# A GpSimd add moved behind the next causal select, and matmuls cut into shorter pieces at two places

## The chip, the cores and the metric

The kernel runs on one core of a Trainium2 chip. The core has five engines that run their own instruction streams and meet at semaphores: TensorE (PE in the rows; PEld is its weight load), VectorE (DVE), ScalarE (ACT), GpSimd (POOL) and SyncE (SP, which here only starts DMAs). The metric is the device time of one execution in microseconds. A run is timed on its own, and one execution is also recorded by the hardware profiler.

## The reference, cut to what matters

Two stages follow each other. The first is attention for 4 batches and 8 heads over 768 positions of 64 numbers, where each query may see 6 of the 24 chunks of 32 keys: those with the highest bound on the score.

```python
ub = np.sum(np.maximum(q * k_min, q * k_max), axis=-1)      # bound of each query on each chunk
ub = np.where(causal, ub, -1e9)
top_chunks = np.argsort(ub, axis=-1)[..., -6:]
scores = scale * np.matmul(q, k.transpose(0, 1, 3, 2))
scores = np.where(sel & (pos[:, None] >= pos[None, :]), scores, -1e9)
attn = np.exp(scores - np.max(scores, axis=-1, keepdims=True))
attn = attn / (np.sum(attn, axis=-1, keepdims=True) + 1e-09)
out = np.matmul(attn, v)
```

The second routes the 3072 rows of 512 to one of 8 experts each (argmax of `x @ w_gate`), keeps at most 80 rows an expert, those with the highest gate, and writes `gate * (relu(x @ w1[e]) @ w2[e])` for the rows kept and zeros elsewhere.

## The kernel before, in words

**Pairs and steps.** Two heads of one batch are worked on together, so there are 16 pairs, `i` = 0 to 15 (`NP` = 16, `NPB` = 4 pairs a batch). The causal half of a pair's score matrix is cut into six steps (`STEPS`). A step is one or two blocks of keys (128 keys on the partitions) against a range of queries (the columns). For each step PE makes the scores (`score_mm`, L572, and L560 for keys in halves of 64) and adds a large negative number for chunks not chosen (`flags`, L594). ACT then takes the exponential out of PSUM into the SBUF buffer `EXB` (L604), and POOL sets the upper triangle of the diagonal block to zero (`select`, L656 or L653).

**Sums.** The softmax denominators come from `ES`, the sum of the exponentials over key blocks. POOL adds step by step (`fold`, L672, with the pieces listed in `ADDS`), and DVE adds a last part (`own_fold`, L678 to L684). `fold(3)` is one add of 512 columns: it sums the step 2 and step 3 exponentials of queries 512 to 767 into `ES`. `sums` (L730, L753) brings `ES` to PSUM on PE once the pair after it has begun, and `sums_out` (L739 to L742) takes reciprocals on DVE.

**Values.** `values` (L717) multiplies the exponentials by `v`: 12 blocks a pair, for each of the two heads, into one PSUM tile `OB`, the heads in its two partition halves. A float32 matmul stands in the trace as two MATMULs and two LDWEIGHTS, so 12 blocks for two heads are 48 MATMULs. In most pairs the order of the blocks is that of `AVS`: the fifth block needs step 4's exponentials after the select, and the last needs step 5's.

**Three kinds of pairs.** `mid(i)` is 1 to 14. `short(i)` holds for 1, 2, 3, 4, 5, 8, 9 and 13: they take keys in halves and run steps 4 and 5 in another order. The other middle pairs are 6, 7, 10, 11, 12 and 14. `direct(i)` holds for 5, 9 and 13. In a short pair `fold(3)` already stands behind step 4's select; in the others it stands right behind step 3's (`folds`, L686 to L701).

**Order.** It is written out by hand: the loop over `i` issues scores, sums of the pair before, folds, values and the preparation of the next pairs, and each engine works through its own list in that order. Routing work of a batch (gates, ranks, tables) is put between the pairs of the next batch, mostly on DVE: in pairs 6, 10 and 14 `rank_hot`, `gate_digits` and the columns of a table (L1072 to L886), whose matmul `table` (L1085) stands in the next pair, for pair 14 in the same pair.

**The end.** For pair 15, `sums_last` (L792) makes the sums straight from `EXB`. The values are given in two calls around `last_row` (L895), which turns the gates for ranking; then counts (L976), the choice of rows, gathers of chosen rows from DRAM by POOL's indirect DMAs (L1366), and the experts' matmuls (L1457 up, L1483 down). The first gathered rows are turned at L1000.

**Splits.** `score_mm` cuts the 512 columns of steps 0 and 1 in two pieces of 256 where `(i - 1) * 2 + st < 10`, that is in pairs 1 to 5.

## Time and profile before

| | |
|---|---|
| time, median of 3 runs | 270.26 us (270.12 to 270.38) |
| the profiled execution | 270.17 us, of which the span of the program's instructions is 268.2 us |
| PE busy | 256.0 us (95%), 4152 MATMULs |
| DVE busy | 214.8 us (80%) |
| POOL busy | 207.6 us (77%) |
| ACT busy | 155.4 us (58%) |
| chain that ended last | PE 73%, POOL 11%, DVE 5%, DMA 4% |

Times in the rows are microseconds from the span's start. In the timeline a row is a run of instructions of one kind: start, length, engine, line, operation, tiles, shapes and count, and in brackets how long the engine sat idle before it and what ended that. PE works on several instructions at a time and the ends of its matmuls are modelled, so its idle time in brackets is a lower bound.

### The profile page before, as it was taken

What the parts mean: (1) busy time and instruction counts of PE and PEld (TensorE: products, weight loads), DVE (VectorE), ACT (ScalarE), POOL (GpSimd) and SP (SyncE); (2) the same over time, 40 slices, a digit from 0 to 9 for tenths busy, and PEclk for the clock granted to TensorE, in tenths of its full rate; (3) what the DMA queues carried; (4) which work ended last, traced back from release to release, by engine and by line L of the source; (5) the groups of instructions that cost most, each with busy time, mean ns of one, the idle gap of its engine ahead of it and who ended that gap; (6) DMA issues with size and microseconds to landing.
All of it is one profiled execution on the core that took longest, in us unless ns stands there. A gap on an engine that the chain in (4) does not pass through costs nothing.

```text
span 268.2 us, 9821 instructions
## 1 busy us (share of the span) xinstructions
PE 256.0 (95%) x4152; PEld 167.2 (62%) x4152; DVE 214.8 (80%) x587; ACT 155.4 (58%) x243; POOL 207.6 (77%) x291
## 2 busy tenths in 40 slices
PE   7799999999999999999999999999999999988993
PEld 7367676767676565666665666666556557664663
DVE  6878787687989988859899889999998998953242
ACT  2286757575777654657776456564865576841220
POOL 6068959895999798969997999888998942725852
PEclk9999999999999999999999999999999999999999
DMA  9979999999999999997999889969999991911771
GB/s 148 173 128 165 142 293 195 298 222 222 151 200 205 226 160 197 206 221 147 164 186 222 150 147 210 212 112 295 287 243 218 215 190 9 197 44 47 152 150 65
DMA packets 148618, 48.38 MB, mean 180 GB/s; under 512 B 131583, under 2 KB 138870, under 8 KB 148512
## 3 DMA queue, kind: packets, MB, share of 16 engines
q1 hardware_dynamic: 113552, 23.23, 44.5%
q0 software_dynamic: 9936, 18.64, 36.9%
q10 hardware_dynamic: 25088, 5.90, 10.9%
q8 instruction: 32, 0.52, 0.8%
q14 instruction: 10, 0.08, 0.1%
HBM read 57.03 MB, written 11.01 MB: 254 GB/s over the span
## 4 chain that ended last, share of the span: by engine, by line
PE 73%; POOL 11%; DVE 5%; DMA 4%; ACT 3%; issue 2%; ACTq 1%; DVEq 0%
PE OB L717 22%; PE SC L572 13%; POOL ES L672 8%; PE SC L560 7%; PE SC L594 5%; PE OB L1483 4%; PE SC L1457 4%; PE MM L483 4%; PE MM L753 3%; ACT EXB L604 3%; DMA qn<-x_rows,idx 3%; PE MM L730 2%; POOL EXB L656 2%; PE OB L801 2%; DMA qn<-in_q_dram 1%
## 5 line engine op out<-in xcount | busy, mean ns | idle before, releaser
L604 ACT ACTIVATE EXB<-SC 128x1024 f32<-128x1024 f32 (+2 forms) x87 | 81.2, 947 | 35.9 <-PE SC L594 14.4
L672 POOL TENSOR_TENSOR ES<-ES,EXB 128x512 f32<-128x512 f32 (+1 forms) x76 | 80.4, 1060 | 5.1
L717 PE MATMUL OB<-EXB,vn 128*64 128x256 f32 (+2 forms) x640 | 69.6, 365 | 0.8 <-POOL EXB L656 0.7
L572 PE MATMUL SC<-qT,kT 64*128 64x256 f32 (+3 forms) x356 | 61.2, 450 | 0.1
L717 PEld LDWEIGHTS OB<-EXB,vn 128*64 128x64 f32 x640 | 42.9, 137 | 23.3 <-issue 7.5
L672 POOL TENSOR_TENSOR ES<-EXB 128x512 f32<-128x512 f32 (+1 forms) x29 | 45.0, 1551 | 1.8
L594 PE MATMUL SC<-unsT,ind 64*128 64x320 bf16 (+9 forms) x286 | 34.9, 303 | 0.4
L572 PEld LDWEIGHTS SC<-qT,kT 64*128 64x128 f32 x356 | 29.1, 187 | 8.9 <-issue 4.4
L725 ACT ACTIVATE oT<-OB 128x512 f32<-128x512 f32 (+1 forms) x32 | 15.7, 490 | 31.6 <-PE OB L717 31.6
L656 POOL TENSOR_SCALAR_AFFINE_SELECT EXB<-EXB 128x256 f32<-128x256 f32 x63 | 27.5, 442 | 5.5 <-ACT EXB L604 5.5
L656 POOL TENSOR_SCALAR_AFFINE_SELECT ES<-EXB 128x256 f32<-128x256 f32 x15 | 7.3, 484 | 22.3 <-PE MM L753 14.9
L594 PEld LDWEIGHTS SC<-unsT,ind 64*128 64x128 bf16 (+1 forms) x286 | 12.3, 100 | 17.9 <-issue 8.2
L560 PE MATMUL SC<-qT,kT 64*64 64x256 f32 (+5 forms) x256 | 21.7, 436 | 0.0
L450 DVE STREAM_TRANSPOSE qT<-qn 128x768 f32<-128x768 f32 x16 | 15.5, 971 | 5.8 <-PE SC L594 5.0
L454 ACT ACTIVATE rq<-qT 128x768 f32<-128x768 f32 x16 | 13.5, 845 | 9.7 <-DVE qT L450 9.2
L460 DVE STREAM_TRANSPOSE kT<-kn 128x768 f32<-128x768 f32 x16 | 15.5, 968 | 1.4 <-DMA kn<-in_k_dram 1.2
L462 DVE TENSOR_REDUCE kmm<-kT 128x24 f32<-128x768 f32 x16 | 15.3, 953 | 0.5
L465 DVE TENSOR_REDUCE kmx<-kT 128x24 f32<-128x768 f32 x16 | 15.1, 941 | 0.0
L497 DVE MAX8 top<-MM 128x8 f32<-128x8 f32 (+4 forms) x160 | 14.6, 164 | 0.6
L828 DVE TENSOR_TENSOR xp<-OB,rden 128x768 bf16<-128x768 f32 x14 | 13.3, 953 | 0.4
L739 DVE STREAM_TRANSPOSE MM<-MM 128x192 f32<-128x192 f32 x16 | 6.3, 394 | 8.3 <-PE MM L753 8.0
L753 PE MATMUL MM<-ES,onc 128*32 128x192 f32 x240 | 12.5, 326 | 0.0
(269 smaller groups left out, 457.4 us busy)
## 6 DMA issues: line engine op xcount, KB each, us to landing
w1s<-in_moe_w_dram POOLq DMA_DIRECT2D x8, 1024.0 KB, 10.0
w2s<-in_moe_w_dram POOLq DMA_DIRECT2D x7, 1024.0 KB, 14.3
kn<-in_k_dram SPq DMA_DIRECT2D x62, 96.0 KB, 3.7
qn<-in_q_dram SPq DMA_DIRECT2D x62, 96.0 KB, 3.9
vn<-in_v_dram ACTq DMA_DIRECT2D x28, 192.0 KB, 4.9
out_dram<-w1s SPq DMA_DIRECT2D x2, 1536.0 KB, 7.3
out_dram<-out_dram SPq DMA_DIRECT2D x2, 1536.0 KB, 9.8
x_rows<-xp SPq DMA_DIRECT2D x7, 384.0 KB, 4.3
```

Source lines behind the costliest of these rows:

```text
L450: op("dve", lambda: ve.transpose(qT[j][:], qn[s][:].rearrange("p a b c -> p (a b c)")), r=[f"qn{s}{g}" for g in range(4)], w=[f"qT{j}"])
L460: op("dve", lambda: ve.transpose(kT[j][:], kn[s][:].rearrange("p a b c -> p (a b c)")), r=[f"kn{s}{g}" for g in range(4)], w=[f"kT{j}"])
L462: op("dve", lambda: ve.tensor_reduce(kmm[j][:, 0, 0:NCH], kv, AX, ALU.min), r=[f"kT{j}"], w=[f"kmm{j}"])
L560: op("pe", lambda: pe.matmul(o, kT[j][pr, k0:k0 + 64], qT[j][pr, q0 + cut:q1], start=not flags, stop=bool(flags)), r=[f"kT{j}", f"qT{j}"], ...
L572: op("pe", lambda: pe.matmul(o, kT[j][pr, ts(kt)], qT[j][pr, x0:x1], start=not flags and (not cols or cols[0] == 0) and n == 0, stop=bool( ...
L594: op("pe", lambda: pe.matmul(ps[ot, h * 512 + c0 + x:h * 512 + c1], ind[pr, k0:k0 + (64 if halves else 128)], unsT[j][pr, b0 - 128 + x:q1 ...
L604: op("act", lambda: ac.activation(Ex(st, None, 0, W, turned(i)), src, ACTF.Exp, scale=SCALE), r=pk, w=[f"E{st}"])
L656: op("gp", lambda: gp.affine_select(ad, a, pattern=[[0, 2], [1, 128]], compare_op=ALU.is_ge, fill=0.0, base=0, channel_multiplier=-1), r=[ ...
L672: op(e, lambda: sy.queue[e].tensor_tensor(o, in0, in1, ALU.add), r=[f"E{s2}", f"E{first[0]}"] if first else [f"E{s2}"] + (["E5"] if (s2, c ...
L717: op("pe", lambda: pe.matmul(OB[pr, q0:q1], vs[:, kt - RT, h, :] if kt >= RT and turned(i) else vn[s][:, kt, h, :], ex, start=(n == 0), st ...
L725: op("act", lambda: ac.activation(oT[:, q0:q1], OB[:, q0:q1], ACTF.Copy), r=[f"O{bk}"], w=[f"oT{bk}"])
L753: op("pe", lambda: pe.matmul(M0[c * 32:c * 32 + 32, 0:192], onc[:, h, :], stripes(ES, h * S + c * 32, 0, 0, None), start=False, stop=(h == ...
```

## The change

Three edits.

1. In `score_mm` the bound 10 becomes 14: the 512 columns of steps 0 and 1 are cut in two pieces of 256 in pairs 6 and 7 as well.
2. In `folds` the add `fold(3)` stands behind step 4's select in all middle pairs, where before it did so in the short ones only. For pairs 6, 7, 10, 11, 12 and 14 it moves past one instruction on POOL.
3. In `values` the blocks of the last pair are cut into pieces of 128 columns, the two heads in turn within a piece.

```diff
@@ score_mm
-                        if st < 2 and mid(i) and (i - 1) * 2 + st < 10:
+                        if st < 2 and mid(i) and (i - 1) * 2 + st < 14:
                             parts = [(q0, q0 + 256), (q0 + 256, q1)]
@@ folds
-                        if short(i) and st == 4:
+                        if mid(i) and st == 4:
                             fold(3, i=i)
-                        if i < NP - 1 and not (short(i) and st == 3):
+                        if i < NP - 1 and not (mid(i) and st == 3):
                             fold(9 - st if st > 3 and short(i) else st, i=i)
@@ values
-                        for h in range(2):
+                        w = 128 if i == NP - 1 else q1 - q0
+                        for x, h in [(x, h) for x in range(0, q1 - q0, w) for h in range(2)]:
                             pr = slice(h * 64, h * 64 + 64)
-                            ex = ES[:, h, 0:128] if st is None else Ex(st, h, c, q1 - q0, short(i))
-                            op("pe", lambda: pe.matmul(OB[pr, q0:q1], vs[:, kt - RT, h, :] if kt >= RT and turned(i) else vn[s][:, kt, h, :], ex,
-                                                       start=(n == 0), stop=last),
+                            ex = ES[:, h, 0:128] if st is None else Ex(st, h, c + x, w, short(i))
+                            op("pe", lambda: pe.matmul(OB[pr, q0 + x:q0 + x + w], vs[:, kt - RT, h, :] if kt >= RT and turned(i) else vn[s][:, kt, h, :], ex,
+                                                       start=(n == 0 and x == 0), stop=last),
...
```

On POOL in pair 6, from the select of step 2 to the first add of `fold(5)`, the kernel before has this order (selects are AFFINE_SELECT, step 5's is the one of 128x256; the adds are TENSOR_TENSOR):

```order
L656 AFFINE_SELECT EXB<-EXB 128x2x128
L672 TENSOR_TENSOR ES<-ES,EXB 128x2x256
L656 AFFINE_SELECT EXB<-EXB 128x2x128
L672 TENSOR_TENSOR ES<-EXB 128x2x256
L656 AFFINE_SELECT EXB<-EXB 128x2x128
L656 AFFINE_SELECT EXB<-EXB 128x256
L672 TENSOR_TENSOR ES<-ES,EXB 128x2x256
```

The changed kernel has this one in the same place:

```order
L656 AFFINE_SELECT EXB<-EXB 128x2x128
L672 TENSOR_TENSOR ES<-ES,EXB 128x2x256
L656 AFFINE_SELECT EXB<-EXB 128x2x128 x2
L672 TENSOR_TENSOR ES<-EXB 128x2x256
L656 AFFINE_SELECT EXB<-EXB 128x256
L672 TENSOR_TENSOR ES<-ES,EXB 128x2x256
```

The selects of steps 3 and 4 now stand together, and the add of `fold(3)` stands between the selects of steps 4 and 5. No DMA start stands between the old and the new place.

On PE near the end, around the two calls of `values` for pair 15, the kernel before has:

```order
L1146 MATMUL MM<-dTb,G 80x5 x8
L717 MATMUL OB<-EXB,vn 64x512 x2
L717 MATMUL OB<-EXB,vn 64x384 x2
L895 MATMUL SC_19<-ident_f,gt_51 128x128 x6
L717 MATMUL OB<-EXB,vn 64x256 x2
L717 MATMUL OB<-EXB,vn 64x128 x2
L717 MATMUL OB<-EXB,vn 64x256 x2
L717 MATMUL OB<-EXB,vn 64x128 x4
L717 MATMUL OB<-EXB,vn 64x256 x6
L717 MATMUL OB<-EXB,vn 64x128 x2
L976 MATMUL MM<-ohb,ES 128x8 x12
```

And the changed kernel, with lines one higher:

```order
L1147 MATMUL MM<-dTb,G 80x5 x8
L718 MATMUL OB<-EXB,vn 64x128 x14
L896 MATMUL SC_19<-ident_f,gt_51 128x128 x6
L718 MATMUL OB<-EXB,vn 64x128 x28
L977 MATMUL MM<-ohb,ES 128x8 x12
```

The 22 matmuls of the last values have become 42, 14 ahead of `last_row` and 28 behind it, with the same columns in sum. In pairs 6 and 7, four times two matmuls of 512 columns have become four times four of 256. DVE, ACT and SP keep their order.

## Rows read from the trace of the kernel before

**Rows 1.** The page: busy time by engine; DMA queues with packets, MB and share.

```profile
PE 256.0 (95%) x4152; PEld 167.2 (62%) x4152; DVE 214.8 (80%) x587; ACT 155.4 (58%) x243; POOL 207.6 (77%) x291
...
q8 instruction: 32, 0.52, 0.8%
```

**Rows 2.** The chain that ended last: start, length, engine, tile, line, count.

```profile
30.34 0.73 PE MM L483 x32
...
36.04 1.06 PE SC L572 x8
...
68.84 0.73 PE MM L483 x32
...
87.85 1.06 PE SC L572 x4
```

**Rows 3.** Timeline of pair 6: step 3's select, values on PE, fold(3), later selects.

```profile
97.38 0.40 POOL L656 TENSOR_SCALAR_AFFINE_SELECT EXB<-EXB 128x256 f32<-128x256 f32 x1
...
97.54 4.84 PE L717 MATMUL OB<-EXB,vn 128*64 128x384 f32 x44
...
97.86 1.28 POOL L672 TENSOR_TENSOR ES<-EXB 128x512 f32<-128x512 f32 x1
...
99.08 0.78 POOL L656 TENSOR_SCALAR_AFFINE_SELECT EXB<-EXB 128x256 f32<-128x256 f32 x2
```

**Rows 4.** Timeline behind pair 6: DVE's last add, a digit of the table, table's load.

```profile
104.16 0.44 DVE L684 TENSOR_TENSOR ES<-ES,EXB 128x256 f32<-128x256 f32 x1 [0.62 <-POOL ES L672]
...
106.03 0.18 DVE L876 CAST gsp<-gdf 128x6 bf16<-128x6 f32 x1
...
108.39 0.30 PEld L1085 LDWEIGHTS MM<-RC,OHS 128*80 128x80 bf16 x6 [0.50 <-DVE lgp L818]
```

**Rows 5.** Timeline of pair 7: exponentials of steps 4, 5; values; POOL's next select.

```profile
110.50 1.30 ACT L604 ACTIVATE EXB<-SC 128x1024 f32<-128x1024 f32 x2 [1.13 <-PE SC L572]
...
111.63 4.49 PE L717 MATMUL OB<-EXB,vn 128*64 128x384 f32 x44
...
120.29 0.41 POOL L656 TENSOR_SCALAR_AFFINE_SELECT ES<-EXB 128x256 f32<-128x256 f32 x1 [1.92 <-PE MM L753]
```

**Rows 6.** Timelines of pairs 10 and 12: values, and two of DVE's instructions.

```profile
152.12 1.90 PE L717 MATMUL OB<-EXB,vn 128*64 128x384 f32 x12
154.17 2.82 PE L717 MATMUL OB<-EXB,vn 128*64 128x128 f32 x32 [0.15 <-POOL EXB L656]
...
180.56 4.67 PE L717 MATMUL OB<-EXB,vn 128*64 128x384 f32 x44
...
180.85 1.21 DVE L870 TENSOR_TENSOR ohb<-oh,lmax 128x48 bf16<-128x48 f32 x1
...
184.65 0.41 DVE L502 TENSOR_TENSOR uns<-MM,top 128x240 bf16<-128x240 f32 x1
```

**Rows 7.** Timeline of pair 14: values in two parts, fold(3), DVE, the table's load.

```profile
208.43 1.89 PE L717 MATMUL OB<-EXB,vn 128*64 128x384 f32 x12
...
209.19 1.28 POOL L672 TENSOR_TENSOR ES<-EXB 128x512 f32<-128x512 f32 x1
...
209.36 1.14 DVE L876 CAST gsp<-gdf 128x6 bf16<-128x6 f32 x1
...
210.88 2.82 PE L717 MATMUL OB<-EXB,vn 128*64 128x128 f32 x32 [0.56 <-POOL EXB L656]
...
213.63 0.30 PEld L1085 LDWEIGHTS MM<-RC,OHS 128*80 128x80 bf16 x6 [0.17 <-DVE uns L502]
```

**Rows 8.** Timeline of the last values, last_row, and the first gathered rows' turn.

```profile
226.38 1.73 PE L717 MATMUL OB<-EXB,vn 128*64 128x512 f32 x8
...
228.33 0.87 PE L895 MATMUL SC<-ident_f,gt 128*128 128x128 f32 x6 [0.22 <-DVE gt L869]
...
229.13 3.25 PE L717 MATMUL OB<-EXB,vn 128*64 128x256 f32 x36
...
235.21 0.32 PE L1000 MATMUL SC<-ident_bf,qn 80*128 80x80 bf16 x4 [0.73 <-DMA qn<-x_rows,idx]
```

## Prediction

> **What bounds the kernel now.** I read the page's engine table first. PE is busy 95% of the span, the next engine 80% [rows 1]. So an edit pays only where it takes away one of PE's few waits, or work that PE does.

> Then I read the chain of waits. Nearly all of it is PE. The 32 matmuls of L483, which stand just ahead of each pair's values, start at 30.34 and, three short pairs later, at 68.84 [rows 2]: 12.83 us a pair. PE itself sets this period.

> Last I read the timeline of each pair that the change touches, for the length of its values. Pair 7 shows the length without a wait: 44 MATMULs in 4.49 [rows 5]. Pair 6 needs 4.84 for the same [rows 3], pair 10 from 152.12 to 154.17 + 2.82 = 156.99, that is 4.87, with an idle time put down to POOL's select [rows 6], pair 12 needs 4.67 [rows 6], and pair 14 from 208.43 to 213.70, that is 5.27, with 0.56 idle ahead of its last 32 [rows 7]. PE stands before step 4's exponentials until POOL has cleared their triangle, and POOL is still in fold(3): in pair 6 the add runs from 97.86 to 99.14 and the select starts at 99.08 [rows 3]. Taken as length over 4.49, the waits are 0.35, 0.38, 0.18 and 0.78, in sum 1.69 us or 0.6% of the time. That is all that edit 2 can remove.

> **Edit 2, pair by pair.** The select moves ahead of an add of 1.28 [rows 3], so PE finds its data. What counts is who is late next.

> *Pairs 6 and 10.* Behind the values, the table's weight load at 108.39 already waits 0.50 for DVE's L818 [rows 4]. DVE's own run there begins at 104.16 with the last add, which waited 0.62 for POOL's add [rows 4]. So PE's 0.35 mostly turns into a longer wait at the table; what stays is what POOL's adds end earlier. Their number is unchanged. Only the handover improves: fold(3) now starts 0.08 behind the end of its own select (97.38 + 0.40 = 97.78 against 97.86), while an instruction that depends on nothing recent starts 0.06 before the end of the one ahead (99.08 against 99.14) [rows 3]. That gives 0.08 + 0.06 = 0.14. I take 0.10 for each of the two, since not every handover need be so; the ends are 0 and the full stalls of 0.35 and 0.38.

> *Pairs 7 and 11.* There is no stall to take away. Here the exponentials of step 4 come late: ACT begins its two of 1024 columns at 110.50 after waiting 1.13 for PE [rows 5]. The moved add must now let POOL stand until they are there, by my reading of about half a microsecond. POOL has 1.92 of idle time before its next pair's select [rows 5], which covers this. If that cover were gone, PE would be late by the 0.5. I take 0.

> *Pair 12.* PE gains 0.18. DVE's L502, on which PE's next transposes stand, ends at 184.65 + 0.41 = 185.06, ahead of the values' end at 185.23 [rows 6], so about this much can be cashed. Besides, fold(3) no longer meets DVE's L870, 1.21 long [rows 6], at the same moment, which can only help L502. I take 0.18; the ends are 0 and 0.23.

> *Pair 14.* PE's stall is the largest, 0.78, but behind the values the load of the table waits until 213.63 for DVE's L502 [rows 7]. DVE is late because a cast of six columns, L876, takes 1.14 beside fold(3) (209.19 to 210.47) [rows 7], where the same cast takes 0.18 in pair 7 [rows 4]. The change moves the add by one select, to about 209.6 to 210.9. It then falls on the instruction behind the cast instead, and DVE is again held until the add is over, 0 to 0.4 later than now. I take 0: PE arrives earlier and waits longer. The ends are a gain of 0.85 (the cast and what follows slip through ahead of the add: 0.78 of stall and nearly all of the 0.17 that the load waits [rows 7]) and a loss of 1.1 (the add at the new place holds one more of DVE's instructions for the 0.8 that it would cost by these rows, and comes 0.3 later).

> [...]

> **Edit 1.** In pairs 6 and 7 it adds 8 matmuls, 16 MATMULs and 16 weight loads. The rows of L572 show both forms: cut in two, 8 MATMULs take 1.06; uncut, 4 take 1.06 [rows 2]. The cost is 0.00 in either direction.

> **Edit 3.** It turns 22 matmuls into 42 with the same columns. Three rows of values give a price: 1.73 for 4 matmuls and 1792 columns, 3.25 for 18 and 3584 [rows 8], 4.49 for 22 and 5120 [rows 5], columns counted for both heads and two MATMULs to a matmul. Differences give 1.52 = 14a + 1792b and 1.24 = 4a + 1536b, so b is 0.79 ns a column and a 8 ns a matmul. Ten more matmuls in each call are 0.08 each. Both stand ahead of waits: `last_row` waits 0.22 for DVE, and the turn of the gathered rows 0.73 for their DMA [rows 8]. The cost is 0; without that cover it is 0.16. The ends of the price itself are 0 (as the split scores show) and this 0.16.

> **Instruction packets.** The page has a queue of 32 instruction packets that hold 16 engines for 0.8% of the span [rows 1]: 0.008 x 16 x 268.2 / 32 = 1.07 us a packet, if all are alike. PE's 4152 MATMULs and as many weight loads [rows 1] are some 260 to a packet, so I estimate that most packets are PE's. The change adds 16 + 40 MATMULs with their loads, 112 instructions in all, so borders in the tail fall 112 earlier in the work, and ahead of the last sums 32 earlier. The even pairs, 12.83 with no regard to where a border falls, show that PE usually has its next instructions in time. I take 0; the ends are one packet more or less in the open, 1.07 either way. That there are fewer records ahead of the last sums, I cannot find: the order shows 32 more.

> [...]

> **The sum** is −0.10 −0.10 −0.18 + 0 + 0 = −0.38 us against the profiled execution's 270.17, of which the span is 268.2. That is 269.79; the median of the runs is 270.26, 0.09 above it, so I forecast 269.88, told as 269.9. Its own range is 269.55 to 270.2.

> **Rivals.**
> - *A: pair 14 cashes its stall too.* DVE gets its cast through before the add, and PE keeps the 0.85. For it: the select, not the add, now stands at the moment when the cast starts. Against: the add follows 0.4 later. 269.9 − 0.85 = 269.0.
> - *B: the moved add holds DVE up in pair 14.* It starts 0.4 later and ends 0.3 to 0.4 later, and if it holds a second instruction, L502 comes 1.1 later and PE with it. For it: L876's 1.14. Against: what follows it is short. It decides once the add holds more than the one instruction. 269.9 + 1.1 = 271.0, slower than before.
> - *C: a packet border falls badly.* Some stretch behind pair 6 that was hidden lies open, or the other way. 269.9 + 1.07 = 270.95, or 269.9 − 1.07 = 268.8.
> - *D: nothing is cashed.* In 6, 10 and 12 another engine is late by as much as PE was, as in pair 14, and the shorter pieces change nothing. Against: pair 12's numbers above. 270.3.

> **How the numbers follow.** Of this kernel a measurement tells some 0.2% from no change, that is 0.54 us: faster is under 269.72, slower over 270.80. Forecast 0.42, of its range about a third (0.13) below 269.72; A 0.22; B 0.10; C 0.10 on the slow and 0.07 on the fast side; D 0.09. Faster: 0.13 + 0.22 + 0.07 = 0.42. The same: 0.29 + 0.09 = 0.38. Slower: 0.20. The range reaches from 268.9, just under A, to 270.95, which takes in half of B and C; outside remain some 0.16.

> **What would show it.** Right: the values of pairs 6, 10, 12 and 14 near 4.49 with no wait for POOL's select; the table's load in pairs 7 and 11 waiting longer than 0.50 for DVE and starting only about 0.1 earlier relative to its pair; L870 in pair 12 a few tenths long; the load of the table in pair 14 still waiting for L502, by more than 0.17; `last_row` waiting 0.14 and the turn of the gathered rows 0.65. Wrong: L502 of pair 14 moved by over 0.3 against its pair's start; a stretch of PE behind 225 that is longer by about a microsecond without a wait shown; the period of pair 6 or 7 changed by the split scores.

## The result, and the profile after

| | before | after |
|---|---|---|
| median (lowest to highest), 22 runs each | 270.44 us (269.96 to 272.3) | 273.06 us (271.17 to 275.11) |
| ratio, 95% interval | | 1.0081 (1.0058 to 1.0104) |
| profiled execution, its span | 270.17 us, 268.2 | 271.37 us, 269.4 |

The changed kernel is slower, and its time varies more: over 3.9 us, against 2.3 before. (The two medians alone stand as 1.0097 to 1.) The forecast was 269.9 us, slightly faster, with 268.9 to 270.95 as its range. The profiled execution is one of the shortest (its mean granted clock is 0.998), so the first comparison shows only a part of the loss.

First the page of the changed kernel, its engines. It answers to [rows 1].

```profile
PE 255.9 (95%) x4208; PEld 171.2 (64%) x4208; DVE 213.3 (79%) x587; ACT 155.6 (58%) x243; POOL 208.3 (77%) x291
```

PE's busy time is the same although it has 56 more MATMULs. So the loss of this execution is waiting. The timeline of PE says where. The rows are the values of pairs 6, 10, 12 and 14 and what follows them in pair 14 (start, length, line, tiles, shapes, count, idle time ahead). They answer to [rows 3, 6, 7].

```profile
97.46 4.49 PE L718 MATMUL OB<-EXB,vn 128*64 128x384 f32 x44
...
151.87 4.49 PE L718 MATMUL OB<-EXB,vn 128*64 128x384 f32 x44
...
180.08 4.49 PE L718 MATMUL OB<-EXB,vn 128*64 128x384 f32 x44
...
207.71 4.49 PE L718 MATMUL OB<-EXB,vn 128*64 128x384 f32 x44
214.74 0.41 PE L1086 MATMUL MM<-RC,OHS 128*80 128x40 bf16 x6 [2.54 <-DVE uns L502]
```

All four waits for step 4's select are gone: each pair takes 4.49. In pair 14, PE then stands idle for 2.54 us until VectorE's L502, where it stood 0.56 and 0.17 before. Until pair 14 the changed kernel was ahead: the values of pair 14 start at 207.71 against 208.43 [rows 7].

Why L502 is late, VectorE's timeline in pair 14 tells, from the gate's first cast to L502:

```profile
208.04 0.37 DVE L875 CAST gsp<-gt 128x6 bf16<-128x6 f32 x1
208.45 0.32 DVE L876 TENSOR_TENSOR gdf<-gt,gsp 128x6 f32<-128x6 f32 x1
208.79 1.22 DVE L877 CAST gsp<-gdf 128x6 bf16<-128x6 f32 x1
210.05 0.32 DVE L878 TENSOR_TENSOR gsp<-gdf,gsp 128x6 bf16<-128x6 f32 x1
...
210.46 2.10 DVE L887 TENSOR_TENSOR RC<-ohb,gsp 128x144 bf16<-128x144 bf16 x1
212.47 0.58 DVE L490 STREAM_TRANSPOSE MM<-MM 128x160 f32<-128x160 f32 x2
...
214.28 0.41 DVE L502 TENSOR_TENSOR uns<-MM,top 128x240 bf16<-128x240 f32 x1
```

And POOL beside it, from the add of fold(2) to the first add behind the DMA start:

```profile
206.32 1.28 POOL L672 TENSOR_TENSOR ES<-ES,EXB 128x512 f32<-128x512 f32 x1
207.55 1.19 POOL L656 TENSOR_SCALAR_AFFINE_SELECT EXB<-EXB 128x256 f32<-128x256 f32 x2
208.72 1.26 POOL L672 TENSOR_TENSOR ES<-EXB 128x512 f32<-128x512 f32 x1
209.94 0.40 POOL L656 TENSOR_SCALAR_AFFINE_SELECT EXB<-EXB 128x256 f32<-128x256 f32 x1
210.30 0.77 POOL L431 DMA_DIRECT2D w2s<-in_moe_w_dram  x1
211.09 1.28 POOL L672 TENSOR_TENSOR ES<-ES,EXB 128x512 f32<-128x512 f32 x1
```

The cast L877 (L876 before) takes 1.22 and is still held until fold(3) ends at 208.72 + 1.26 = 209.98, as it was before (1.14, [rows 7]). New is the product L887: it takes 2.10. It starts at 210.46, inside POOL's DMA start, and ends at 212.56, that is 0.19 after the first add behind the DMA start (211.09 + 1.28 = 212.37). In the kernel before, the same product (L886) started 0.30 ahead of that DMA start and took 0.50. VectorE's rows there, and POOL's from fold(2) on (fold(3) stands between them, [rows 7]):

```profile
209.16 0.17 DVE L875 TENSOR_TENSOR gdf<-gt,gsp 128x6 f32<-128x6 f32 x1
...
210.94 0.50 DVE L886 TENSOR_TENSOR RC<-ohb,gsp 128x144 bf16<-128x144 bf16 x1
```

```profile
207.04 1.28 POOL L672 TENSOR_TENSOR ES<-ES,EXB 128x512 f32<-128x512 f32 x1
...
210.43 0.86 POOL L656 TENSOR_SCALAR_AFFINE_SELECT EXB<-EXB 128x256 f32<-128x256 f32 x2
211.24 0.77 POOL L431 DMA_DIRECT2D w2s<-in_moe_w_dram  x1
```

### The profile page after: what moved, and what is told of

Same layout as the page of the kernel before. It is cut to its first block, busy times and chain, and to the rows that moved or that the text cites. A ratio compares the mean times of both kernels' runs of the same rounds, so it can differ in the third digit from the quotient of the medians.

```text
span 269.4 us, 9933 instructions
## 1 busy us (share of the span) xinstructions
PE 255.9 (95%) x4208; PEld 171.2 (64%) x4208; DVE 213.3 (79%) x587; ACT 155.6 (58%) x243; POOL 208.3 (77%) x291
## 4 chain that ended last, share of the span: by engine, by line
PE 73%; DVE 8%; POOL 8%; DMA 4%; ACT 4%; issue 1%; ACTq 1%; DVEq 0%
PE OB L718 21%; PE SC L572 13%; PE SC L560 7%; POOL ES L672 6%; PE SC L594 5%; PE OB L1484 4%; PE SC L1458 4%; PE MM L483 4%; PE MM L754 3%; ACT EXB L604 3%; DMA qn<-x_rows,idx 2%; PE MM L731 2%; PE OB L802 2%; DMA qn<-in_q_dram 1%; PE MM L521 1%
## 5 line engine op out<-in xcount | busy, mean ns | idle before, releaser
L718 PE MATMUL OB<-EXB,vn 128*64 128x128 f32 (+2 forms) x680 | 68.7, 352 | 0.0
L572 PE MATMUL SC<-qT,kT 64*128 64x256 f32 (+3 forms) x372 | 61.3, 438 | 0.1
L718 PEld LDWEIGHTS OB<-EXB,vn 128*64 128x64 f32 x680 | 45.0, 137 | 19.9 <-issue 7.3
L572 PEld LDWEIGHTS SC<-qT,kT 64*128 64x128 f32 x372 | 30.6, 187 | 9.1 <-issue 4.4
L656 POOL TENSOR_SCALAR_AFFINE_SELECT ES<-EXB 128x256 f32<-128x256 f32 x15 | 6.6, 440 | 21.5 <-PE MM L754 14.0
```

The costliest lines, as they stand in the source:

```text
L572: op("pe", lambda: pe.matmul(o, kT[j][pr, ts(kt)], qT[j][pr, x0:x1], start=not flags and (not cols or cols[0] == 0) and n == 0, stop=bool( ...
L656: op("gp", lambda: gp.affine_select(ad, a, pattern=[[0, 2], [1, 128]], compare_op=ALU.is_ge, fill=0.0, base=0, channel_multiplier=-1), r=[ ...
L718: op("pe", lambda: pe.matmul(OB[pr, q0 + x:q0 + x + w], vs[:, kt - RT, h, :] if kt >= RT and turned(i) else vn[s][:, kt, h, :], ex, start= ...
```

## The experiments

Theory 1: in pair 14 the moved add makes VectorE late, VectorE makes PE wait, and the lower clock comes with that wait. Theory 2: the pieces of the last values and the packet borders cost the time in the tail. In each, the ratio is to runs of the kernel before on the same chip.

**again**: the changed kernel, no edit.

> The changed kernel once more, nothing altered. It shows how its time and its granted clock vary from one execution to the next: 271.2 to 275.1 us so far, with a mean granted clock of 0.998 where it took 271.4 and 0.987 to 0.993 where it took 273 to 275. Theory 1 (PE's long wait for VectorE in pair 14 costs 1.8 us by itself, and the lower clock comes with it): a profile of one of the longer executions would show the granted clock low somewhere behind that wait, from 213 on. Theory 2 (the lower clock comes from the tail, where the last values are in pieces): it would be low only behind 226. Both expect 271 to 275.

Measured: 272.94 us median (271.25 to 274.13), ratio 1.0084 (1.0054 to 1.0114). The profiled execution took 274.13 us, with a mean granted clock of 0.987. Its windows from the end of pair 14's values on (stretch, length, busy times of PE, PEld, DVE, ACT, POOL, then PEclk, DMA share, GB/s):

```profile
212.00:214.50 2.50, 0.21 (x4) 0.00 (x0) 2.40 (x15) 0.38 (x1) 2.33 (x3) 1.00 0.99 189
214.50:221.30 6.80, 6.58 (x36) 3.41 (x36) 3.44 (x10) 2.62 (x3) 1.91 (x3) 0.50 0.75 161
221.30:226.00 4.70, 4.66 (x58) 2.68 (x58) 3.54 (x10) 3.05 (x6) 0.86 (x2) 1.00 0.00 0
```

The granted clock is 1.00 through most of PE's idle stretch and falls to 0.50 at its end, at about 214.5, for 6.8 us. Below, the first scores behind it and the row where the clock is back, in this execution:

```profile
215.91 2.08 PE L572 MATMUL SC<-qT,kT 64*128 64x512 f32 x4
...
221.43 0.53 PE L777 MATMUL MM<-kT,wg 128*32 128x192 f32 x8
```

and in the execution profiled first, which kept 1.00 there:

```profile
215.48 1.13 PE L572 MATMUL SC<-qT,kT 64*128 64x512 f32 x4
...
218.40 0.53 PE L777 MATMUL MM<-kT,wg 128*32 128x192 f32 x8
```

Both have the table's first matmul at 214.7; at L777 they differ by 221.43 − 218.40 = 3.03 us. So in this execution the clock is low behind the wait and back at 1.00 before the last values: theory 2's place is excluded for it.

**all_but14**: pair 14's fold(3) back in its old place.

```diff
-                        if mid(i) and st == 4:
+                        if mid(i) and i < NP - 2 and st == 4:
                             fold(3, i=i)
-                        if i < NP - 1 and not (mid(i) and st == 3):
+                        if i < NP - 1 and not (mid(i) and i < NP - 2 and st == 3):
```

> The changed kernel with pair 14's fold(3) alone back in its old place, right behind step 3's select. Theory 1: PE's wait behind pair 14's values falls from 2.54 back to about 0.75 and the time to 270.3 - 0.7 = 269.6 us (the 0.7 being what the changed kernel had gained by pair 13), with a clock near 1.00 in nearly every run. Theory 2 (pieces and packet borders in the tail cost the time and the clock): it stays between 271 and 275, with the clock as low as in the changed kernel.

Measured: 269.42 us (269.2 to 269.93), ratio 0.9974 (0.996 to 0.9987), clock 1.000. Theory 1 holds. With one add in one pair put back, PE's wait there is 0.54, the loss becomes a gain of 0.46 us by the medians (269.88 for the kernel before), and the spread is gone.

**only14**: the kernel before, with that one move.

```diff
-                        if short(i) and st == 4:
+                        if (short(i) or i == NP - 2) and st == 4:
                             fold(3, i=i)
-                        if i < NP - 1 and not (short(i) and st == 3):
+                        if i < NP - 1 and not ((short(i) or i == NP - 2) and st == 3):
```

> The kernel before with pair 14's fold(3) alone moved behind step 4's select. Theory 1: VectorE is blocked twice (the cast of 6 columns 1.1 to 1.2 us, the column product 2 us instead of 0.5), PE waits about 2.5 us, and the time is 270.3 + 1.8 = 272 us or more, with a lower clock in many runs, up to 275. Theory 2: no change or a gain by the removed 0.78 us wait, 269.5 to 270.3, and a clock of 1.00.

Measured: 273.32 us (271.54 to 274.68), ratio 1.0113 (1.0078 to 1.0149). PE's wait in pair 14, and the window of the low clock behind it (columns as above):

```profile
215.24 0.41 PE L1085 MATMUL MM<-RC,OHS 128*80 128x40 bf16 x6 [2.49 <-DVE uns L502]
```

```profile
212.20:215.80 3.60, 1.11 (x22) 0.76 (x20) 3.33 (x17) 0.38 (x1) 3.37 (x4) 1.00 1.15 231
215.80:219.20 3.40, 3.40 (x20) 1.50 (x16) 2.44 (x8) 1.42 (x2) 1.02 (x2) 0.50 0.97 191
```

The move alone makes the whole loss. The product L886 takes 2.08 there, and starts 0.17 behind the DMA start.

**no_move**: the changed kernel without edit 2 (both lines of `folds` as before).

```diff
-                        if mid(i) and st == 4:
+                        if short(i) and st == 4:
```

> The changed kernel without edit 2: no fold(3) is moved, while the scores of pairs 6 and 7 are cut and the last values are in pieces. Theory 1: 270.3 us within 0.3, as the prediction had it for edits 1 and 3. Theory 2: 272 to 274 us, with the lower clock.

Measured: 269.79 us (269.43 to 270.0), ratio 0.9985 (0.9971 to 0.9998). Edits 1 and 3 cost nothing; by the interval they may give a little. The time lies 0.2 under the expected 270.3 ± 0.3; the kernel before, measured beside it, took 269.88. Its trace shows the last values in 28 and 56 MATMULs:

```profile
226.10 1.75 PE L718 MATMUL OB<-EXB,vn 128*64 128x128 f32 x28
...
228.86 3.28 PE L718 MATMUL OB<-EXB,vn 128*64 128x128 f32 x56
```

They stand for 1.73 and 3.25 [rows 8]: 0.05 us in all for 20 more matmuls.

**filler**: the changed kernel, PE kept busy through the wait.

```diff
                     values(i)
                     if i == NP - 2:
+                        for n in range(4):
+                            pr = slice(n % 2 * 64, n % 2 * 64 + 64)
+                            op("pe", lambda: pe.matmul(SC[0][:, n % 2 * 512:n % 2 * 512 + 512], kT[0][pr, 0:128], qT[0][pr, 0:512], start=True, stop=True),
+                               r=["kT0", "qT0"], w=["SC0"], inc=n == 3)
                         table(bb)
```

> The changed kernel with 4 more score matmuls of 512 columns on PE right behind pair 14's values; their result is overwritten unread. By the rows of L572 they take 2.1 to 2.3 us, so they fill the wait of 2.54 us and move nothing else. Theory 1a (the granted clock falls because PE stands idle there): the clock stays at 1.00 in nearly every run and the time is that of the changed kernel's best runs, 271.2 to 271.6, instead of a median of 273. Rival 1b (the clock falls by something else in this stretch, or by chance): the clock is low in as many runs as before and the median stays at 273, or above it.

Measured: 271.03 us (270.97 to 271.3), ratio 1.0039 (1.0024 to 1.0054). PE in pair 14:

```profile
212.14 1.99 PE L1321 MATMUL SC<-qT,kT 64*128 64x512 f32 x8
214.73 0.41 PE L1086 MATMUL MM<-RC,OHS 128*80 128x40 bf16 x6 [0.60 <-DVE uns L502]
```

The table starts where it did (214.74), and the product still takes 2.09, so up to there only PE's idleness was changed, and with it the low clock and the spread went: the clock is 0.997 or more in all 6 runs. In late14, measured on the same chip with the wait open, it is 0.987 to 0.994 in 5 of 6. The wait, with the gains of the other pairs set against it, is worth 1.0039; the clock is the rest of the 1.0081 to 1.0084.

**w2late**: w2's load of pair 14 started behind fold(5).

```diff
                         select(i, st)
-                        if i == NP - 2 and st == (4 if short(i) else 5):
-                            wload(E - 2, 1)
...
                             fold(9 - st if st > 3 and short(i) else st, i=i)
+                        if i == NP - 2 and st == (4 if short(i) else 5):
+                            wload(E - 2, 1)
```

> The changed kernel with the start of w2's load in pair 14 moved behind fold(5). It asks what held the column product L887 for 1.5 us too long (from 210.46 to 212.56 in the trace of the changed kernel): POOL's DMA start at 210.30 (0.77) with the add at 211.09 behind it, or an add alone. If the DMA start took part, L887 now meets the add alone and takes 1.1 to 1.6, and PE's wait falls by 0.5 to 0.9: 270.5 to 272. If not (it was the add alone, recorded too late), it takes about as long or is held by the second add: no change, 271 to 274.

Measured: 271.91 us (270.42 to 272.28), ratio 1.0062 (1.0039 to 1.0086). The product, with the adds now from 210.31 on, and PE's wait:

```profile
210.45 1.38 DVE L887 TENSOR_TENSOR RC<-ohb,gsp 128x144 bf16<-128x144 bf16 x1
```

```profile
214.02 0.40 PE L1086 MATMUL MM<-RC,OHS 128*80 128x40 bf16 x6 [1.82 <-DVE uns L502]
```

L887 is 0.72 shorter and so is PE's wait (2.54 to 1.82), about the length of the DMA start (0.77). So the DMA start took part: in the changed kernel the product waited through it (0.77), and the next add (1.28) then went ahead.

**late14**: pair 14's fold(3) behind step 5's select and w2's load.

```diff
-                        if mid(i) and st == 4:
+                        if mid(i) and st == (5 if i == NP - 2 else 4):
                             fold(3, i=i)
```

> The changed kernel with pair 14's fold(3) moved one place further, behind step 5's select and the start of w2's load. [...]

Measured: 272.86 us (271.09 to 273.95), ratio 1.0098 (1.0069 to 1.0128). I had expected 269.4 − 0.5 = 268.9 if L877 and L887 ran clear of the add, which failed; the rival was that POOL's selects and DMA starts hold the two as well, so that one of them stays at 1 us or more, for 269.5 to 272. L887 did stay at 1.39, and an instruction between the two, L878, met the DMA start and took 2.00. The time lies above the rival's range (PE waits 2.63, and the clock is 0.987 to 0.994 in 5 of 6 runs). VectorE:

```profile
208.79 0.34 DVE L877 CAST gsp<-gdf 128x6 bf16<-128x6 f32 x1
209.16 2.00 DVE L878 TENSOR_TENSOR gsp<-gdf,gsp 128x6 bf16<-128x6 f32 x1
...
211.25 1.39 DVE L887 TENSOR_TENSOR RC<-ohb,gsp 128x144 bf16<-128x144 bf16 x1
```

POOL:

```profile
209.05 0.77 POOL L431 DMA_DIRECT2D w2s<-in_moe_w_dram  x1
209.84 1.29 POOL L672 TENSOR_TENSOR ES<-EXB 128x512 f32<-128x512 f32 x1
```

The cast is free now (0.34). The next instruction, which took 0.32 in the changed kernel, starts at 209.16 inside the DMA start and ends at 211.16, as the add behind it ends (209.84 + 1.29 = 211.13): the pattern of L887 once more, on another instruction. L887 itself starts at 211.25, 0.05 behind the start of the add that follows fold(3) (211.20), and takes 1.39.

**digits13**: digits and products of the last table on VectorE in pair 13.

```diff
+                    if i == NP - 3:
+                        gate_digits(bb)
+                        gate_cols(bb)
+                        gate_gcols(bb)
...
                     if i == NP - 2:
-                        rank_late(bb)
+                        rank_hot(bb)
```

> The changed kernel with the gate's digits and both column products of the last table (L875 to L887) issued in pair 13 on VectorE, not in pair 14. Theory 1: with them gone from the stretch where fold(3) now stands, only the one-hot compare L1077 can meet an add; L502 comes 2 us earlier and PE's wait in pair 14 is below 0.3: 268.7 to 269.3, if pair 13 hides six short instructions on VectorE (about 2 us by their unblocked lengths; if it doesn't, up to 1 us more). Rival (PE's wait comes from something else than these instructions, such as POOL's later adds): the wait stays above 1.5 us and the time above 271.

Measured: 270.32 us (270.09 to 270.94), ratio 1.0011 (0.9999 to 1.0023). In pair 14, PE no longer waits for L502 (it ends at 211.87 + 0.41). But the six instructions take VectorE from 203.25 to 206.40 in pair 13, so what follows them is some 3 us late, and PE waits at another place, ahead of pair 14's values:

```profile
207.76 0.79 PE L483 MATMUL MM<-qT,kmm 64*32 64x160 f32 x9 [0.96 <-POOL ES L672]
```

The row names POOL's add; VectorE's L819, which reads the same tile, ended at 207.61, about when that add did, so which of the two let PE go isn't settled. That the held instructions make PE's wait in pair 14 is confirmed; the expected 268.7 to 269.3 is missed, since pair 13 didn't hide the six instructions.

**digits_late**: VectorE's chain for PE first, digits behind it; the table behind pair 15's first scores.

```diff
                         bounds_out(i + 1)
+                    if i == NP - 2:
+                        gate_digits(bb)
+                        gate_cols(bb)
+                        gate_gcols(bb)
...
-                    scores(i, 0, 2 if i else 3)
+                    scores(i, 0, 1 if i == NP - 1 else 2 if i else 3)
                     if i == NP - 1:
+                        table(bb)
+                        merge(bb)
+                        scores(i, 1, 2, False)
```

(`rank_late` keeps `rank_hot` alone, and the calls of `table` and `merge` behind pair 14's values are dropped.)

> The changed kernel, fold(3) moved in pair 14 too, with VectorE's chain that PE waits for (L490 to L502) ahead of the digits and column products, and the last table's matmuls behind pair 15's first scores instead of right behind pair 14's values. Theory 1 (PE's wait is the held instructions ahead of L502, nothing else): L502 ends near 210.8, PE goes on at 212.2 without a wait and the clock stays at 1.00; the table then waits for the digits, held by adds, for 0 to 2 us behind the first scores: 268.5 to 270.5 us. Rival (pair 14's move has another price, in POOL's adds or the sums): 271 or more.

Measured: 271.67 us (270.44 to 273.95), ratio 1.006 (1.0029 to 1.0092). The median lies above the expected 268.5 to 270.5, in the rival's range, and the clock is 0.987 to 0.994 in 6 of 12 runs. PE goes on behind the values at 212.20 without a wait, as expected. Then the wait comes back in two places:

```profile
214.93 0.41 PE L1086 MATMUL MM<-RC,OHS 128*80 128x40 bf16 x6 [1.09 <-DVE RC L887]
...
217.56 1.29 PE L1122 MATMUL OB<-ident_f,gT 80*80 80x80 f32 x8 [0.97 <-DVE gT L1108]
```

The digits are held as before (the last of the six, L887, takes 1.40 and ends at 214.88), so the table can't come before 214.9. The one that starts inside the DMA start (210.47, 0.77 long here) takes 2.00 instead of 0.32:

```profile
210.58 2.00 DVE L876 TENSOR_TENSOR gdf<-gt,gsp 128x6 f32<-128x6 f32 x1
```

In this execution the clock is 0.50 from 217.60 to 220.90, behind the second wait.

**digits_late_old**: the same, pair 14's fold(3) in its old place (edit as in all_but14).

> The same new place of digits and table, with pair 14's fold(3) left in its old place. PE keeps the wait of 0.54 for step 4's select in pair 14, and L502 is then early. Theory 1: 0.3 to 0.6 us above digits_late, if the digits are held alike in both; 268.9 to 270.5. If the two are equal or this one is faster, the removed wait of pair 14 is not to be cashed even with L502 early.

Measured: 270.93 us (270.77 to 271.05), ratio 1.0025 (1.0013 to 1.0038), clock 1.000. The table starts at 214.90, within 0.03 of digits_late. The stall that the move removes (0.52) is followed by a wait that is longer by 0.68 (1.09 against 0.41): in pair 14 it can't be cashed as long as the digits end when they do. My expectation that this one would be slower failed, and so did its 268.9 to 270.5.

**move_mid**: the kernel before, with fold(3) moved in pairs 6, 7, 10, 11 and 12 only (the condition of all_but14).

> The kernel before with fold(3) moved in pairs 6, 7, 10, 11 and 12 alone: edit 2 without pair 14, and without edits 1 and 3. The prediction's sum for it is -0.38 us against the kernel before. If edits 1 and 3 cost and give nothing, it equals all_but14 against its own runs of before (-0.46 there): -0.3 to -0.5. If edits 1 and 3 gave the part by which the changed kernel without edit 2 was ahead (-0.09), it is -0.3 to -0.4.

Measured: 269.43 us (269.27 to 270.6), ratio 0.9974 (0.9958 to 0.9991). It is as fast as all_but14 (both 0.9974). These two and, by little, no_move (0.9985) are the versions that beat both kernels.

## Why the prediction was wrong, point by point

**Pair 14, the step that failed.** The prediction took 0 for it, on the ground that VectorE "is again held until the add is over, 0 to 0.4 later than now". That much came: counted from the start of fold(2) (207.04 before, 206.32 after), fold(3) starts 0.25 later (2.15, then 2.40). It did not fall on the instruction behind the cast, though. The subtraction ahead of the cast took 0.32 instead of 0.17 and ended with the second select, so the cast came 0.15 later and still found the add under way.

What the step left out is what POOL's order puts behind the add. Between fold(3) and w2's DMA start only step 5's select is left, where two selects stood. So, again counted from fold(2), that DMA start comes 0.22 earlier (4.20, then 3.98), while VectorE's product, behind the held cast, comes 0.24 later (3.90, then 4.14). The product, which had been 0.30 ahead of the DMA start, now began 0.16 behind it. DMA start and next add together cost it 2.10 − 0.50 = 1.60 us; with the 0.24 that is 1.84, and PE's wait grew by 2.54 − 0.56 − 0.17 = 1.81. The prediction's own sign of being wrong, L502 over 0.3 late against its pair's start, came with 1.83: L502 starts 4.74 behind the values before (213.17 − 208.43) and 6.57 after (214.28 − 207.71).

Rival B, with a chance of 0.10, had the right engine, pair and sign; its mechanism (a second instruction under the moved add) was nearly right, but the second was held by a DMA start and another add. Its price of 1.1 was too low.

What held VectorE here, the rows show by length. The cast took 1.22 beside the moved add, and 0.34 beside selects alone (late14). Three subtractions or products (L887, L878, L876) that began inside a DMA start in pair 14 took 1.99 to 2.10, and the first took 1.38 when the DMA start was moved away (w2late); another instruction (L1077, in the last section) kept its length of 0.66. Why the two cases differ isn't shown.

**The granted clock, which no case had.** The prediction reckoned with a wait as time lost once. A run whose wait of 2.5 us is followed by 3.4 or 6.8 us at a granted clock of 0.50 loses 3.0 more for the longer of these (again), and most runs lose some: 20 of 29 have a clock of 0.994 or less. Filled with unread work, the same wait costs 1.0039; open, 1.0081. That PE's idleness brings the low clock there is shown by filler (0.997 or more in 6 of 6 runs, against 0.987 to 0.994 in 5 of 6 of late14); in w2late 1.82 us of it still did so in 5 of 6 runs (0.993 or 0.994). It isn't the only occasion: the kernel before has such runs too (0.994 and 271.15 to 271.79 us in 6 of the 29 beside the last three experiments), and no profile of one is on record. What decides between a run that keeps 1.00 and one that does not is open: digits_late_old, whose waits of 0.52, 0.41 and 0.97 are apart, stayed within a spread of 0.3 us, while digits_late with 1.09 and 0.97 did not.

**Pairs 6, 10 and 12: right as to their sum.** It was −0.38 us. Measured are −0.37 (all_but14 against no_move, 269.42 − 269.79) and, for move_mid, 269.43 − 270.05 = −0.62 by the medians, or 0.24 to 1.1 less by the interval of its ratio. How it is shared out differs. The values of pairs 10, 12 and 14 in no_move start at:

```profile
152.02 4.82 PE L718 MATMUL OB<-EXB,vn 128*64 128x384 f32 x44
...
180.41 4.57 PE L718 MATMUL OB<-EXB,vn 128*64 128x384 f32 x44
...
208.19 1.89 PE L718 MATMUL OB<-EXB,vn 128*64 128x384 f32 x12
```

The changed kernel's start 0.15, 0.33 and 0.48 earlier. So by these two executions the places in pairs 6 and 7 gave 0.15, those in 10 and 11 0.18 and that in 12 0.15, where 0.10, 0.10 and 0.18 were taken. In pair 6 the table's load now waits longer, as predicted, and starts 0.26 earlier, of which 0.08 was there at the start of the pair's values:

```profile
108.13 0.30 PEld L1086 LDWEIGHTS MM<-RC,OHS 128*80 128x80 bf16 x6 [0.66 <-DVE lgp L819]
```

against 0.50 and 108.39 [rows 4]. In pair 12 the product that took 1.21 [rows 6] takes 0.23.

**Pairs 7 and 11: right.** In pair 7 the moved add lets POOL wait 0.65 (0.5 predicted), and its idle time ahead of the next pair's select shrinks from 1.92 [rows 5] to 1.42; in pair 11 it waits 0.61, and the idle time shrinks from 1.66 to 0.56. No run moved these two alone.

```profile
111.33 0.41 POOL L656 TENSOR_SCALAR_AFFINE_SELECT EXB<-EXB 128x256 f32<-128x256 f32 x1 [0.65 <-ACT EXB L604]
...
120.03 0.41 POOL L656 TENSOR_SCALAR_AFFINE_SELECT ES<-EXB 128x256 f32<-128x256 f32 x1 [1.42 <-PE MM L754]
```

**Edits 1 and 3: right as to the sum** (no_move). The price of a matmul was taken as 8 ns and is 0.05 us / 20 = 2.5 ns. The wait at `last_row` is 0.20 to 0.21 where 0.14 was predicted. In the changed kernel the turn of the gathered rows waits 0.33 instead of the predicted 0.65; why the gathers land earlier relative to PE's work, no run here asks:

```profile
235.86 0.32 PE L1001 MATMUL SC<-ident_bf,qn 80*128 80x80 bf16 x4 [0.33 <-DMA qn<-x_rows,idx]
```

**Packets: 0 was right as far as the runs show.** The page of the changed kernel has 33 instead of 32. No trace here shows where a packet's border falls or what one costs; the 1.07 us was an estimate from the page. no_move, with the same added matmuls, took 269.79 against 269.88, which leaves no room for that much in the open.

## What to carry to other kernels

A wait removed on the bound engine is worth what the next engine lets through: here 0.91 us of waits in pairs 6, 10 and 12 became a gain of 0.37 (all_but14 against no_move). Before moving an instruction on GpSimd, lay its new row, and the rows behind it, which move too (adds and DMA starts alike), beside VectorE's rows at that time. Look for every short instruction that would start inside one; here that cost the rest of the one (the cast took 1.22 instead of 0.34) and, behind the DMA start, the whole of the next (the product took 2.10 instead of 0.50). Where VectorE then makes TensorE idle for as long as here (1.82 to 2.63 us), add what a fall of the granted clock costs behind it (up to 3.0 us in again), and read the spread of the runs before the profile of one. Try such a move pair by pair: the other five places together gave 0.4 to 0.6 us, and the sixth cost more than that.

## What the runs showed of the hardware that was not expected

```profile
104.11 0.78 POOL L428 DMA_DIRECT2D w1s<-in_moe_w_dram  x1
104.88 0.75 POOL L431 DMA_DIRECT2D w2s<-in_moe_w_dram  x1
```

VectorE beside them:

```profile
104.59 0.66 DVE L1077 TENSOR_TENSOR OHS<-iota,rk 128x480 bf16<-128x480 f32 x1
105.16 0.47 DVE L875 CAST gsp<-gt 128x6 bf16<-128x6 f32 x1
```

The compare L1077 starts 0.48 into the first and goes on into the second, at its shortest length (0.66 of 0.66 to 1.55 in this trace); the cast L875 starts 0.28 into the second and ends with it. Whether the place inside the DMA start decides, or the add right behind it, no run asks.

The clock did not fall at the start of PE's idle stretch but near its end or behind it: at about 214.5 where PE went on at 214.72 (again), at about 215.8 where it went on at 215.24 (only14). It stayed at 0.50 for 6.8 and 3.4 us, with PE busy for 6.58 and 3.40 of them.
